# A fused delta-rule attention and GELU feed-forward kernel, rebuilt: batches in partition halves, a Newton inverse, 512-token feed-forward groups, casting weight loads

## The chip, the cores and the metric

The kernel runs on one core of a Trainium2 chip. The metric is the device time of one execution in microseconds (us). "Slower", "faster" and "same" compare it with the kernel before on the same chip. All profile times are from the start of the profiled span.

## The reference

Two stages follow each other. `q`, `k`, `v` are `[4, 8, 768, 48]` (batch, head, position, head size), `beta` is `[4, 8, 768]`.

```python
k_n = k / (np.linalg.norm(k, axis=-1, keepdims=True) + 1e-06)
for t in range(S):                          # state: [B, H, 48, 48], zero at first
    y[:, :, t] = einsum('bhd,bhde->bhe', q[:, :, t], state)
    v_old = einsum('bhde,bhd->bhe', state, kt)
    state = state + bt * einsum('bhd,bhe->bhde', kt, vt - v_old)
x = y.transpose(0, 2, 1, 3).reshape(3072, 384)
h = x @ w_in                                # [384, 2048]
g = 0.5 * h * (1 + tanh(c * (h + 0.044715 * h**3)))
out = g @ w_out                             # [2048, 384]
```

Both kernels cut the 768 positions into 12 chunks of 64. Within a chunk the recurrence is a triangular system: with the strictly lower matrix A of `beta_i k_i.k_j`, the updates of a chunk are `U = (I + A)^-1 (beta V - beta K state)`, the new state is `state + K^T U`, and the output is `Q state + tril(Q K^T) U`.

## The kernel before, in words

Work is cut into 24 units. Unit `u` is chunk `u // 2` of two of the four batches, so 16 (batch, head) pairs, laid out as 8 column groups on two partition halves of 64 (`pairs`, L293): the two halves hold two heads of one batch. Matrices of one pair are 64x64, so nearly every matmul uses one 64x64 tile of TensorE, and two of them run side by side on the diagonal tiles.

A unit has three parts, all in functions of the kernel's body:

- `prep(u)` (L398): POOL squares `k`, takes the norm (`pow`, L415), scales `k` by it and by `beta` (L411 to L427); TensorE turns the three 64x64 blocks of a pair (48 transposes, L435), DVE copies them out (L438); `gram2` and `gram` (L455, L448) form the triangular matrices, which DVE masks (L462, L466). The inverse of `I + A` is a product of `I + A^(2^i)`: L474 to L541 square a matrix five times and apply it, with three right-hand blocks in `mnl`, `m4`, `n4`, `m5` and `lt`. `wmat` (L543) makes `beta K` times the inverse.
- `chain(u)` (L554): the serial part, from one chunk's state to the next: `umat` (L566), `smat` (L584), the state's sum (L594), `omat` (L597). The output comes out with head dimension on partitions, 48 of each 64; six small DMAs on SP's queue (L616) move the fourth group of heads into the 16 free rows, so that `xo` holds the 384 features as three blocks of 128.
- `mlp(u)` (L620): for 128 tokens, 48 matmuls of 128 columns against `W1` (L633), GELU on ACT (L638, four 512-column pieces), 16 matmuls of 384 columns against `W2` (L645), a copy and two output DMAs.

`W1` and `W2` come in float32 through two staging buffers `wst` on SP's queue (L381) and are cast by ACT or DVE (L386) into bf16. `load(c)` (L361) brings a chunk of `k`, `q`, `v` for all four batches; three buffers (`NR`). Five `prep` buffers (`NP`), four of `xo` (`NX`).

The order is made by a planner in `Flow.schedule` (L70): each operation has an estimated duration and a key (its due time in units, `prep` at `u`, `chain` at `u - 0.5`, `mlp` from `u + 2.5`). The planner simulates the engines, takes at each free engine the ready operation with the lowest key, places PSUM tiles in 8 banks, and so fixes every engine's queue; `emit` (L167) writes the queues with semaphore waits. TensorE's queue is in order: an operation that waits holds all behind it.

Of the kernel before, what the change touches and what calls it, by code (L numbers as in the profile page):

```python
# [8 lines left out]
BF16 = mybir.dt.bfloat16  # L9
ALU = mybir.AluOpType  # L10
# [8 lines left out]
class Op:  # L19
    __slots__ = ("engs", "fn", "dur", "key", "deps", "alloc", "frees", "mode", "dma", "users", "missing",  # L20
                 "on", "t0", "t1", "tag", "clock", "bankdeps", "seq")


class Flow:
# [3 lines left out]
    LAT = {"pe": 0.20, "dve": 0.08, "act": 0.08, "pool": 0.10}  # L28
    SWITCH = 0.095
    SLACK = 0.6  # L30
    DMA_LAT = 2.2

# [7 lines left out]
    def add(self, eng, fn, dur, reads=(), writes=(), key=0.0, alloc=None, accum=(), frees=(), mode=None, dma=None):  # L40
        o = Op()
        o.engs = (eng,) if isinstance(eng, str) else tuple(eng)
        o.fn, o.dur, o.key, o.mode, o.dma = fn, dur, key, mode, dma
# [6 lines left out]
        for name in o.frees:  # L50
            self.left[name] += 1
# [18 lines left out]
    def schedule(self):  # L70
# [17 lines left out]
        events, t, done, mode, dma_free = [], 0.0, 0, None, 0.0  # L88

# [6 lines left out]

        def choose(e):
            held, pick = [], None
            while ready[e]:
                item = heapq.heappop(ready[e])  # L100
                o = item[2]
                if o.on is not None:
                    continue
                held.append(item)
                if pick is not None and item[0] - pick[0] > self.SLACK:
                    break
                if o.alloc and place(o.alloc[1]) is None:
                    continue
                if e != "pe" or o.mode == mode:
                    pick = item  # L110
                    break
                if pick is None:
                    pick = item
            for item in held:
                if item is not pick:
                    heapq.heappush(ready[e], item)
            return pick[2] if pick else None

        while done < len(self.ops):
            for e in ENGINES:  # L120
                while free[e] <= t + 1e-9:
# [5 lines left out]
                    if e == "pe" and o.mode != mode:  # L127
                        d += self.SWITCH
                        mode = o.mode
# [6 lines left out]
                    if o.dma is not None:  # L136
                        dma_free = max(dma_free, t + 0.65) + d
                        free[e], o.t1 = t + 0.65, dma_free + self.DMA_LAT
# [8 lines left out]
            while True:  # L147
                if o is not None:
                    done += 1
                    for name in o.frees:  # L150
                        self.left[name] -= 1
                        b = self.at[name]
                        for x in range(b, b + self.size[name]):
                            last[x].append(o)
                            if not self.left[name]:
                                bank[x], since[x] = None, t
# [8 lines left out]
        self.t_end = t  # L165

    def emit(self, nc, psum):  # L167
        count, total, names = {e: 0 for e in ENGINES}, {}, list(ENGINES)
        last_done, groups = {}, {}
# [12 lines left out]
        plan = {e: [] for e in ENGINES}  # L182
        for o in sorted(self.ops, key=lambda o: (o.t0, o.seq)):
            e, mine = o.on, known[o.on]
            need = {}
            for d in o.deps | o.bankdeps:
                if d.on == e and d.dma is None and (e == "pe" or self.only_war(o, d)):
                    continue
# [44 lines left out]
    def only_war(self, o, d):  # L233
        return False


def bass_deltanet__then__act_gelu_tanh_kernel(
# [12 lines left out]
    NC, FC, G, J = S // C, FF // 128, 8, 4  # L250
    NU = 2 * NC
    DP = 112
# [4 lines left out]
    with nc.allow_non_contiguous_dma("strided loads"), nc.allow_low_precision("bf16 pipeline"):  # L257
# [5 lines left out]
        NR, NP, NX = 3, 5, 4  # L263
        ident = sb("ident", [128, 128], F32)
        id64 = sb("id64", [128, C])
        mfull = sb("mfull", [128, 2, 128], F32)
        mneg = sb("mneg", [128, C], F32)
        mup = sb("mup", [128, 2, C], F32)
        half = sb("half", [128, G], F32)
        braw = sb("braw", [32, NC, 2, C], F32)  # L270
        bsb = sb("bsb", [128, NC, 2 * G], F32)
        raw = {n: sb(n + "raw", [128, 2 * G, D], F32, NR) for n in "kvq"}
        sq = sb("sq", [128, G, D], F32)
        nrm = sb("nrm", [128, 4, G], F32, NP)
        kn, kb, qb = (sb(n, [128, G, C], BF16, NP) for n in ("kn", "kb", "qb"))
        vb = sb("vb", [128, G, D], BF16, NP)
        kT = sb("kT", [128, 3, G, C], BF16, NP)
        mnl = [sb(f"mnl{i}_", [128, 3, G, C], BF16, NP) for i in range(3)]
        m4, n4, m5, lt = (sb(x, [128, G, C], BF16, NP) for x in ("m4", "n4", "m5", "lt"))
        wn = sb("wn", [128, G, C], BF16, NP)  # L280
        us = sb("us", [128, G, D], BF16, 3)
        st = sb("st", [128, G, D], BF16, 4)
        xo = sb("xo", [128, J, 128], BF16, NX)
        gT = sb("gT", [128, FC, 128], BF16, 3)
        ob = sb("ob", [128, DM], F32, 2)
        W1 = sb("W1", [128, 3, FF])
        W2 = sb("W2", [128, FC, DM])
        wst = sb("wst", [128, FF], F32, 2)

        def half_rows(a, n=C):  # L290
            return slice(64 * a, 64 * a + n)

        pairs = [(g, a) for g in range(G) for a in range(2)]  # L293
        PEO, T1, T2 = 0.05, 0.0165, 0.029


        def const():
            A("pool", lambda e, P: e.memset(ident[:, :], 0.0), 0.2, writes=["ident"])
            A("pool", lambda e, P: e.affine_select(out=ident[:, :], in_=ident[:, :], compare_op=ALU.not_equal, fill=1.0,
                                                   base=0, pattern=[[-1, 128]], channel_multiplier=1), 0.4,  # L300
              reads=["ident"], writes=["ident"])
            A("pool", lambda e, P: e.memset(half[:, :], 0.5), 0.1, writes=["half"])
            A("pool", lambda e, P: e.memset(mfull[:, :, :], -1.0), 0.3, writes=["mfull"])
            for x, cm in ((0, 1), (1, -1)):
                A("pool", lambda e, P, x=x, cm=cm: e.affine_select(
                    out=mfull[:, x, :], in_=mfull[:, x, :], compare_op=ALU.is_gt, fill=0.0, base=0,
                    pattern=[[-cm, 128]], channel_multiplier=cm), 0.4, reads=["mfull"], writes=["mfull"])
            for a in range(2):
                r = half_rows(a)
                A("dve", lambda e, P, r=r: e.tensor_copy(id64[r, :], ident[r, r]), 0.15, reads=["ident"],  # L310
                  writes=[f"id64{a}"])
                A("dve", lambda e, P, r=r: e.tensor_copy(mneg[r, :], mfull[r, 0, r]), 0.25, reads=["mfull"], writes=[f"mneg{a}"])
                A("dve", lambda e, P, r=r: e.tensor_copy(mup[r, 0, :], mfull[r, 1, r]), 0.25, reads=["mfull"], writes=[f"mupa{a}"])
                A("dve", lambda e, P, r=r: e.tensor_scalar(mup[r, 1, :], mfull[r, 1, r], -1.0, None, op0=ALU.mult), 0.2,
                  reads=["mfull"], writes=[f"mupb{a}"])

        ID = ["id640", "id641"]
        MNEG, MUP = ["mneg0", "mneg1"], ["mupa0", "mupa1", "mupb0", "mupb1"]
# [4 lines left out]
        def ev(n, wide=False):  # L323
            return {"act": 0.18 + 0.00083 * n, "dve": 0.14 + (0.00053 if wide else 0.00104) * n}

        EV = ("act", "dve")
        PAD = lambda s: [f"pad{s}", f"pad{s}.1", f"pad{s}.2"]

        def warm_up():
            wz = sb("wz", [128, 128])  # L330
# [371 lines left out]
```

## Time and profile before

| what | value |
|---|---|
| three runs | 385.56, 392.3, 393.79 us (median 392.3) |
| profiled execution | 392.4 us span |
| TensorE matmuls in it | 10,020, each with a weight load |
| granted TensorE clock, mean | 0.970 |
| HBM read, written | 20.55 MB, 4.72 MB |

PE is TensorE's matmul, PEld its weight load, DVE is VectorE, ACT ScalarE, POOL GpSimd, SP SyncE. A busy digit is tenths of a slice. The end of a matmul is modelled, so the time from the start of one operation to the start of the next is the better price of a matmul on a full TensorE. The queue row "instruction" is the fetching of program code: most of its packets hold 16,384 bytes.

### The profile page before, as it was taken

The numbers are of one execution on the slowest core, as the hardware profiler recorded it, in microseconds if no ns is written. First come the engines' busy times: TensorE is split into PE (matmuls) and PEld (weight loads), VectorE is DVE, ScalarE is ACT, GpSimd is POOL, SyncE is SP. The second block draws the span as 40 slices with busy tenths as digits, with TensorE's granted clock in tenths as the row PEclk, the third lists the DMA queues.
The fourth block names the chain that finished last, engine by engine and source line by source line (L and its number), as shares of the span: only waits on it lengthen the run. The fifth ranks groups of instructions, "written<-read, shape, count | busy, mean of one in ns | idle before, by whom it ended". The sixth has DMA issues, their size and how long they took to land.

```text
span 392.4 us, 21411 instructions
## 1 busy us (share of the span) xinstructions
PE 333.6 (85%) x10020; PEld 277.5 (71%) x10020; DVE 234.0 (60%) x387; ACT 188.2 (48%) x327; POOL 165.8 (42%) x203
## 2 busy tenths in 40 slices
PE   4346846867999999988988998999998998999966
PEld 4346845756778777767776787788877886887744
DVE  6756836746767576474664773776577565556300
ACT  1034326456555545545544455556635664564522
POOL 8973733769688318234434436343322211011000
PEclk9999968899999999998999999999999999999988
DMA  9999996890651163053035033010111110101110
GB/s 141 169 163 160 176 187 97 159 190 12 161 113 39 24 107 65 8 103 64 6 71 90 15 67 67 5 28 7 25 26 26 26 23 7 28 6 39 31 24 20
DMA packets 86600, 27.23 MB, mean 69 GB/s; under 512 B 81008, under 2 KB 86128, under 8 KB 86128
## 3 DMA queue, kind: packets, MB, share of 16 engines
q1 hardware_dynamic: 82816, 25.18, 36.0%
q8 instruction: 78, 1.28, 1.4%
q10 hardware_dynamic: 3696, 0.69, 1.2%
q14 instruction: 10, 0.08, 0.1%
HBM read 20.55 MB, written 4.72 MB: 64 GB/s over the span
## 4 chain that ended last, share of the span: by engine, by line
PE 63%; issue 9%; DVE 8%; POOL 7%; SPq 6%; DMA 5%; ACT 2%; ACTq 0%; POOLq 0%
PE ps L633 14%; PE ps L645 13%; PE ps L493 7%; SPq L616 5%; PE ps L487 5%; PE ps L435 4%; POOL nrm L415 3%; PE ps L524 3%; PE ps L478 3%; PE ps L451 2%; DMA xo<-xo 2%; DMA kraw<-in_k_dram 2%; PE ps L572 2%; PE ps L458 2%; PE ps L545 2%
## 5 line engine op out<-in xcount | busy, mean ns | idle before, releaser
L633 PE MATMUL ps<-xo,W 128*128 128x128 bf16 x1152 | 81.3, 224 | 11.5 <-DMA xo<-xo 7.7
L638 ACT ACTIVATE gT<-ps 128x512 bf16<-128x512 f32 x96 | 57.3, 597 | 70.2 <-PE ps L633 69.0
L633 PEld LDWEIGHTS ps<-xo,W 128*128 128x128 bf16 x1152 | 69.7, 100 | 20.2 <-DMA xo<-xo 9.2
L645 PE MATMUL ps<-W,gT 128*128 128x384 bf16 x384 | 77.8, 329 | 0.0
L321 ACT ACTIVATE mnl<-ps 128x512 bf16<-128x512 f32 (+1 forms) x75 | 52.8, 710 | 48.1 <-PE ps L478 28.7
L470 POOL TENSOR_TENSOR mnl<-mnl,id 128x512 bf16<-128x512 bf16 x24 | 27.7, 1156 | 105.9 <-DVE mnl L466 102.7
L493 PE MATMUL ps<-mnl 64*64 64x128 bf16 x1152 | 49.0, 228 | 7.1 <-issue 6.0
L321 DVE CAST mnl<-ps 128x512 bf16<-128x512 f32 (+1 forms) x45 | 33.0, 734 | 30.5 <-PE ps L487 17.3
L415 POOL TENSOR_TENSOR nrm<-nrm,half 128x8 f32<-128x8 f32 x24 | 39.8, 1658 | 13.9 <-DVE nrm L413 13.8
L493 PEld LDWEIGHTS ps<-mnl 64*64 64x64 bf16 x1152 | 38.2, 115 | 8.9 <-issue 7.0
L645 PEld LDWEIGHTS ps<-W,gT 128*128 128x128 bf16 x384 | 31.3, 98 | 17.3 <-issue 0.5
L539 DVE TENSOR_TENSOR lt<-ps,lt 128x384 bf16<-128x384 f32 (+1 forms) x48 | 23.4, 488 | 31.8 <-PE ps L524 31.1
L518 DVE TENSOR_TENSOR mnl<-ps,mnl 128x512 bf16<-128x512 f32 x48 | 32.9, 686 | 9.6 <-ACT mnl L321 9.3
L487 PE MATMUL ps<-mnl 64*64 64x64 bf16 (+1 forms) x1152 | 32.9, 198 | 4.5 <-ACT mnl L321 2.4
L427 POOL TENSOR_TENSOR vb<-vraw,bsb 128x384 bf16<-128x384 f32 x23 | 20.0, 869 | 35.8 <-PE ps L577 29.7
L487 PEld LDWEIGHTS ps<-mnl 64*64 64x64 bf16 x1152 | 26.1, 115 | 9.0 <-ACT mnl L321 2.3
L466 DVE TENSOR_TENSOR mnl<-ps,mup 128x1024 bf16<-128x1024 f32 x24 | 29.2, 1219 | 0.7 <-PE ps L451 0.6
L438 DVE COPY kT<-ps 112x1536 bf16<-112x1536 bf16 x24 | 22.8, 952 | 8.0 <-PE ps L435 7.9
L524 PE MATMUL ps<-lt,m 64*64 64x48 bf16 (+1 forms) x768 | 21.5, 187 | 6.3 <-issue 5.8
L411 POOL TENSOR_TENSOR sq<-kraw 128x384 f32<-128x384 f32 x22 | 18.7, 849 | 15.5 <-DMA kraw<-in_k_dram 15.5
L524 PEld LDWEIGHTS ps<-lt,m 64*64 64x64 bf16 x768 | 17.2, 113 | 11.1 <-issue 8.0
L420 POOL TENSOR_TENSOR kn<-kraw,nrm 128x384 bf16<-128x384 f32 x23 | 19.1, 828 | 11.6 <-DVE nrm L419 9.3
(82 smaller groups left out, 551.1 us busy)
## 6 DMA issues: line engine op xcount, KB each, us to landing
out_dram<-ob SPq DMA_DIRECT2D x48, 96.0 KB, 2.4
kraw<-in_k_dram SPq DMA_DIRECT2D x22, 192.0 KB, 5.5
qraw<-in_q_dram SPq DMA_DIRECT2D x22, 192.0 KB, 5.6
vraw<-in_v_dram SPq DMA_DIRECT2D x22, 192.0 KB, 4.7
wst<-in_moe_w_out_dram SPq DMA_DIRECT2D x4, 768.0 KB, 5.9
wst<-in_moe_w_in_dram SPq DMA_DIRECT2D x6, 384.0 KB, 7.4
xo<-xo SPq DMA_DIRECT2D x144, 4.0 KB, 2.2
wst<-in_moe_w_in_dram SPq DMA_DIRECT2D x6, 128.0 KB, 8.1
```

Of the source, the lines that this page charges most:

```text
L321: return e.activation(out, in_, ACT.Copy) if e is nc.scalar else e.tensor_copy(out, in_)
L415: A("pool", lambda e, P: e.tensor_tensor(nr[:, 1, :], nr[:, 0, :], half[:, :], ALU.pow), 1.65, reads=[n("nrm"), "half"], writes=[n("nrm")] ...
L466: A("dve", lambda e, P: e.tensor_tensor(z0[:, 1:3, :, :].rearrange("p x g t -> p g x t"), P(ps("G")).rearrange("p (g x t) -> p g x t", x=2 ...
L470: A("pool", lambda e, P: e.tensor_tensor(z1[:, 2, :, :], z0[:, 1, :, :], id64[:, :].unsqueeze(1).to_broadcast([128, G, C]), ALU.add), 1.16 ...
L487: ins = e.matmul(cols(P, name, 0, g, w)[r, :], z[r, 1, g, :], z[r, 0, g, 0:w])
L493: ins = e.matmul(cols(P, name, 0, 2 * g, 2 * C)[r, :].rearrange("p (x t) -> p x t", x=2), z[r, 0, g, :], z[r, 1:3, g, :])
L518: A("dve", lambda e, P, z=z, pn=pn, lout=lout: e.tensor_tensor(lout, g2(P, pn, 1), z[:, 2, :, :], ALU.add), 0.69, reads=[n(zn + "l"), afte ...
L524: ins = e.matmul(cols(P, name, 0, g, C - lo, lo)[r, :], m[r, g, :], lt[s][r, g, lo:C])
L539: A("dve", lambda e, P, lo=lo, pl=pl: e.tensor_tensor(lt[s][:, :, lo:C], P(pl).rearrange("p (g t) -> p g t", g=G)[:, :, lo:C], lt[s][:, :, ...
L633: ins = e.matmul(P(ph)[:, 128 * f:128 * f + 128], W1[:, t, 128 * (i + f):128 * (i + f) + 128], x_[:, t, :], start=(t == 0), stop=(t == 2))
L638: A("act", lambda e, P, i=i, ph=ph: e.activation(g_[:, i:i + 4, :].rearrange("p f t -> p (f t)"), P(ph), ACT.Gelu_apprx_tanh), 0.62, frees ...
L645: ins = e.matmul(P(po)[:, 0:DM], g_[:, f, :], W2[:, f, :], start=(f == 0), stop=(f == FC - 1))
```

## The change

The new kernel computes the same with the same 24 units and the same planner class.

- **Layout.** A partition half is now a batch, the free dimension holds the 8 heads. A pair of heads lies side by side in 128 columns, so one 128x128 transpose turns two heads of two batches: 12 instead of 48 (L446). `gram`, `gram2` and the products with the state use all four 64x64 corners of the array (`quad`): a head's parity picks the row half, the batch the column half.
- **Inverse.** The power product is replaced by five Newton steps, X <- X(2I - LX), each two products: the first with -L (or its transpose, in turn), to which DVE adds 2I (L515), the second with X, and a copy of the result (L520). In steps 1 and 3 (`WIDE`) the two halves are one block-diagonal 128x128 operand, `bd`, filled by POOL (two `affine_select` in step 1, two copies in step 3) and used by 8 matmuls instead of 16. Masking is by `copy_predicated` (L474, L478) onto preset buffers. `wmat`, the apply steps and POOL's L470 are gone.
- **Chain.** `K state` is subtracted from `v` by DVE (L550), then `umat` multiplies with the inverse; `Q state` and the inner product share a PSUM tile `O` of two banks. The output has tokens on partitions; three 128x128 transposes (L596) put the features there. The six copying DMAs are gone.
- **Feed-forward.** Tokens are taken in groups (`GROUPS`): chunks 0, 1, 10 and 11 alone (256 tokens), the others two by two (512 tokens). An up matmul has 256 or 512 columns; a GELU instruction covers 1,024 columns, two PSUM banks.
- **Weights.** Four DMAs on POOL's queue cast float32 to bf16 on the way; W1's wait for chunk 0's `v`, W2's for chunk 1's `v`. The staging buffers and the 24 casts go.
- **Planner.** It models code blocks of 256 instructions with a refill of 4.2 us, gives ACT first call on the copies that DVE could also do, and makes POOL wait between operations on different partition halves. The clearing of PSUM by DVE (L656, 3,472 ns) goes, and TensorE's warm-up is 24 matmuls of 512 columns.

```diff
-        pairs = [(g, a) for g in range(G) for a in range(2)]
+        quad = [(p, a) for a in range(2) for p in range(2)]
+    WIDE = (1, 3)
+    GROUPS = [[0], [1]] + [[c, c + 1] for c in range(2, NC - 2, 2)] + [[NC - 2], [NC - 1]]
...
+                A("pool", lambda e, P, f0=f0: e.dma_start(W1[:, :, f0:f0 + FF // 2], w1v[:, :, f0:f0 + FF // 2]), 7.0,
+                  reads=["vraw01"], writes=[f"W1{i}"], dma=f"w1{i}", key=-3 + 0.1 * i)
...
+                for y in range(3):
+                    for g in range(4):
+                        c0 = 512 * y + 128 * g
+                        ins = e.transpose(t[:, c0:c0 + 128], tok[s][:, y, 2 * g:2 * g + 2, :]..., ident[:, :])
...
+            def gram(e, P):
+                for g in range(4):
+                    for p, a in quad:
+                        r = hf(p, D)
+                        o = P(ps("G"))[hf(a), 512 * p + 128 * g:512 * p + 128 * g + 128]
+                        ins = e.matmul(o..., kT[s][r, 1, g, hf(a)], kT[s][r, 0:3:2, g, hf(a)])
...
+            A("dve", lambda e, P: e.copy_predicated(
+                wp[s][:, :, :], mup[:, :].bitcast(U16).unsqueeze(1).to_broadcast([128, H, 2 * C]),
+                P(ps("G")).rearrange("p (h t) -> p h t", h=H)), 1.24, ...)
...
+            for i in range(1, 6):
+                def product(e, P, name, cur=cur, wide=wide, rhs=None):
+                    for h in range(H):
+                        o = P(name)[:, C * h:C * h + C]
+                        if wide:
+                            ins = e.matmul(o, bd[s][:, h, :], rhs[:, h, :])
+                        else:
+                            for a in range(2):
+                                ins = e.matmul(o[hf(a), :], cur[hf(a), h, :], rhs[hf(a), h, :])
...
+                A("dve", lambda e, P, i=i: e.tensor_tensor(rt[s], P(ps(f"A{i}")), two, ALU.add), 0.71, ...)
...
-            for t in range(3):
                 for a in range(2):
-                    A("sp", lambda e, P, t=t, a=a: e.dma_start(x_[64 * a + 48:64 * a + 64, t, :],
-                                                               x_[64 * a + 16 * t:64 * a + 16 * t + 16, 3, :]),
...
+            def trans(e, P):
+                for j in range(J):
+                    ins = e.transpose(P(ps("X"))..., xb[:, 128 * j:128 * j + 128], ident[:, :])
...
+            nf = 1024 // w
+            for i in range(0, FC, nf):
+                def up(e, P, i=i, ph=ph):
+                    for f in range(nf):
+                        for j in range(J):
+                            ins = e.matmul(P(ph)[:, w * f:w * f + w], W1[:, j, 128 * (i + f):...], x_[:, j, 0:w], ...)
```

Line numbers of the new functions are those of the changed kernel.

649 lines of the change are left out of this document (309 added, 340 removed).

## The prediction

> **What bounds the kernel now.** I read the page's busy line and slices first, then the busy times by stretch, then TensorE's timeline inside one stretch, last the chain of work.
>
> ```profile
> PE 333.6 (85%) x10020; PEld 277.5 (71%) x10020; DVE 234.0 (60%) x387; ACT 188.2 (48%) x327; POOL 165.8 (42%) x203
> ...
> PE   4346846867999999988988998999998998999966
> ...
> DMA  9999996890651163053035033010111110101110
> ...
> q8 instruction: 78, 1.28, 1.4%
> ```
>
> TensorE is the only engine that fills slices, and only from 100 us on. Before that the DMA engines are full and TensorE is not.
>
> ```profile
> 0.00:60.00 60.00, 32.96 (x987) 30.42 (x988) 38.43 (x63) 15.79 (x26) 41.48 (x74) 0.94 1.07 167
> 60.00:100.00 40.00, 29.86 (x1009) 26.44 (x1010) 25.07 (x46) 22.97 (x40) 26.25 (x26) 0.91 0.63 117
> 100.00:240.00 140.00, 129.35 (x3842) 104.94 (x3838) 88.78 (x154) 71.10 (x126) 66.70 (x71) 0.99 0.34 65
> 240.00:360.00 120.00, 116.20 (x3763) 96.38 (x3760) 76.59 (x117) 65.37 (x114) 31.36 (x35) 1.00 0.10 21
> 360.00:392.40 32.40, 25.23 (x439) 19.35 (x437) 5.14 (x8) 13.00 (x24) 0.00 (x0) 0.89 0.12 27
> ```
>
> Columns: stretch, PE, PEld, DVE, ACT, POOL busy with counts, clock, DMA share, GB/s. A unit has 416 matmuls (272 prep, 80 chain, 64 feed-forward). From 240 to 360 us 3,763 matmuls are 9.05 units: 13.26 us a unit, with TensorE busy 97%. At that rate 24 units are 318 us; the other 74 us of the span are lost: in the first 100 us only 1,996 matmuls run (4.8 units, worth 64 us, so 36 lost), from 100 to 240 some 18 (3,842 are 9.2 units, 122 us), the rest at the end.
>
> ```profile
> 252.07 0.83 PE L633 MATMUL ps<-xo,W 128*128 128x128 bf16 x12
> 252.84 0.42 PE L524 MATMUL ps<-lt,m 64*64 64x32 bf16 x16
> 253.11 0.42 PE L487 MATMUL ps<-mnl 64*64 64x64 bf16 x16
> 253.36 0.61 PE L493 MATMUL ps<-mnl 64*64 64x128 bf16 x16
> 253.81 0.40 PE L545 MATMUL ps<-lt,kb 64*48 64x64 bf16 x16
> 254.14 0.82 PE L645 MATMUL ps<-W,gT 128*128 128x384 bf16 x4
> 254.80 0.83 PE L633 MATMUL ps<-xo,W 128*128 128x128 bf16 x12
> ...
> 256.84 0.38 PE L587 MATMUL ps<-us,kn 64*48 64x48 bf16 x16
> ```
>
> Start to start gives the prices: 16 diagonal matmuls of 64 columns 0.25 us, of 128 columns 0.45 to 0.49, 12 full ones of 128 columns 0.77 (64 ns each), 4 of 384 columns 0.66 (0.43 ns a column). The smallest group, L587, takes 0.22 until 257.06.
>
> ```profile
> 25.77 4.47 issue
> ...
> 49.62 5.78 issue
> ...
> 378.65 1.71 DMA xo<-xo
> ```
>
> In the chain of work, "issue" is TensorE waiting for nothing that the profile names. The queue "instruction" moved 78 packets for 20,040 matmuls and loads, 257 a packet, and 30 packets in the 120 us from 240 on: one in 4.0 us. I read the issue pieces as waits for code behind the full DMA engines. The last line is the end: the copy of heads inside `xo`, waited out by the last unit.
>
> **The change part by part.** All per unit, on TensorE, at the prices above.
> - *Transposes*: 48 small ones (0.76) become 12 full ones, 12 x 64 ns = 0.77.
> - *Grams*: 0.25 + 0.45 before. Now four corners. The warm-up (L338) is the only row of that: 20 matmuls of 64 columns on the diagonal in 5.26:5.77 (0.51 us), then 34 counted on four corners in 5.77:6.11 (0.34). So corners cost between half and all of the diagonal; I take 0.26 for each gram (half of 0.49 for 128 columns, and for 64 columns no better than the diagonal), 0.52; upper end 0.74.
> - *Inverse*: before 0.51 (L478) + 3 x (0.26 + 0.49) + 0.27 + 2 x 0.34 + 0.33 = 4.0. Now 6 narrow products of 16 x 64 columns, 6 x 0.26 = 1.56, and 4 wide ones of 8 matmuls with a full weight load and 64 columns. No row has that shape: at half of the full 128-column matmul 8 x 32 ns = 0.26, at the whole of it 0.51. I take 0.27, since a wide one streams half the columns and L633's loads already keep pace with 64 ns; 1.08, upper end 2.04. Sum 2.64.
> - *Chain*: before 0.53 + 0.22 + 0.55 = 1.30. Now two products with the state (0.22 each by L587), `umat` and `omat` 0.26 each, `smat` 0.22, three transposes 0.20: 1.38; nothing saved. The six DMAs go. They cost SP 0.59 us each and 1.71 until landing at the end, and hold up the up matmuls 9.2 us in the list of waits.
> - *Feed-forward*: up 4 x 0.77 = 3.08 before. Now 48 matmuls of 512 columns at 0.43 ns, 10.6 us for four units, 2.65; with 256-column groups the same. Down unchanged, 4 x 0.68 = 2.72. The whole gain of the wide groups is 0.4.
>
> Sum now 0.77 + 0.52 + 2.64 + 1.38 + 5.37 = 10.7, against 12.6 for the old parts by the same prices. The old kernel needed 13.26, that is 1.05 times, for waits; 10.7 x 1.05 = 11.2. Twenty-four units: 270 us against 318.
>
> *Code*: 6,828 matmuls instead of 10,020 (255 a unit outside the feed-forward, 768 in it, 36 at the start), 53 packets; one in 5.0 us of TensorE's work instead of 4.0. The Trainium skill, "Runtime: NRT & Kernel Launch", "Instruction fetch mechanics", holds that fetching is hidden behind the issue of instructions. Here it is not (4.47 and 5.78 us above), so a shorter program is worth something.
>
> A rule against the change: the Trainium skill, "TensorE: Matmul & The Clock Gate" ("Wait — 56ns, not 53.3ns?"), says that matmuls never start closer than about 25 ns. By it the 240 small matmuls of a unit would take 6.0 us instead of 4.3, and the estimate from that page is 40 us more, 355. L487's 16 in 0.25 us are 16 ns apart, so I sum by the row.
>
> *Other engines, per unit.* DVE: reduce 0.53, two small ones 0.4, kT 0.95, masks, five sums with 2I at 0.69 (L518's size) = 3.4, two chain sums 1.1. For `copy_predicated` the trace has no row; L462 and L466 read the same PSUM tiles and take 0.69 and 1.22. Below that I see no reason to go, since the reads are the same; above, twice: 1.9 to 3.8; I take 1.9. DVE 8.3 us of 11.2. ACT: GELU 2 x 1.02 (a 128x1024 ACTIVATE takes 1,024 ns), copies 5 x 0.60 + 4 x 0.49: 7.0, of which DVE takes some. POOL: 0.85 + 1.64 + 0.83 + 0.83 + 0.58, two `affine_select` of 512 elements (128 elements took 0.28 to 0.59; 0.6 to 2.0 each, I take 0.9) and two copies (0.4 each): 7.3, at most 10. All lie beside TensorE; if TensorE were free, DVE would be next at some 10 us with its share of the copies. What is late behind them is hidden by five prep buffers: a unit's five Newton steps are 5 x (0.26 + 0.2 + 0.7 + 0.26 + 0.2 + 0.6) = 11 us and POOL's fills, some 25 us from norm to inverse, against 5 x 11.2.
>
> *The start.* The loads are as many bytes, 9.8 MB up to three chunks and both weights, at 167 GB/s 59 us. In the old kernel the weights queue behind chunks on SP and behind two staging buffers: the last cast of W is at 111 us, and SP issues the first `xo` copies only at 56 us for an `omat` of 44 us, so the first up matmul is at 78 us. Now weights run on their own queue, W1 at some 30 to 40 us, W2 by 60. POOL's presets (15 small memsets 0.2, eight to ten selects, some 13 us) come ahead of its first `pow`, which was at 6.9 us; the first unit's transposes slip from 14 to some 18, its inverse to 40, feed-forward from about 48 us. Until then TensorE has four units' prep, some 17 us of work, and a wait for code or two. Lost: 34 us, then no more than the 5%.
>
> W1's and W2's waits stand in POOL's queue: if chunk 1's `v` lands late, `pow` and the scalings of the next units stand behind W2's issue, and TensorE has nothing to do but W1's matmuls. The planner lets W1 go first, so some 5 us of that are in the 34.
>
> *The end.* After the last matmul 0.49 us of copy and the output DMA, 3.7 us as before (388.7 to 392.4). The last group's feed-forward is counted above; its last GELU and the chain ahead of it leave TensorE waiting some 3 us, and part at half clock as before (0.89 over 360:392). 7 us, against the old 11.
>
> Sum: 270 + 34 + 7 = 311, and 4 for copies that come late with DVE at three quarters: 315. The profiled execution's own span is 392.4, the median of the runs 392.3, so nothing is added.
>
> **The rivals.**
> - *VectorE becomes the bound.* If `copy_predicated` costs twice and DVE takes two copies a unit: 8.3 + 1.9 + 1.3 = 11.5, at 95% 12.1 x 24 = 290, from 15 us on, plus 18 for the last group's feed-forward and output, plus 15 of waits in the chain: 338. For it: DVE has 76.6 of 120 us now and gets more; against: ACT is at 65 and gets first call on the copies.
> - *TensorE's pieces are dearer:* wide products and corners at their upper ends, 10.7 + 0.96 + 0.22 + 0.2 = 12.1 x 1.05 x 24 = 305, + 45 = 350.
> - *Little is lost*: no waits in the steady part (257), 28 at the start, 7: 292.
> - *Slower: casting loads land late.* No casting DMA is in the trace. Nearest are the rows of W's loads (768 KB in 5.9 us) and the 4-byte packets, some 10 ns each, a bound of a few GB/s if a cast moved single elements. Before W2 lands, TensorE can do the chains of chunks 0 to 3 (three `xT` buffers), five units' prep and two groups of up matmuls, some 75 us. Then 195 us remain and 7 at the end: the old time is reached when W2 lands at 190 us, 6.3 MB at under 36 GB/s from 15 us on; +2% at 198. Against: 167 GB/s with 192-byte packets. The Trainium skill, "DMA: Bandwidth & Descriptors" ("SWDGE vs HWDGE vs iDMA"), adds that such loads have their descriptors written by GpSimd into SBUF, which DVE can lock out; no run here shows it.
>
> **How the numbers follow.** TensorE-bound as summed, 298 to 330: 0.57. Little lost: 0.12. VectorE or dear pieces, 330 to 360: 0.22. Late weights 0.09, of which 0.04 beyond 400 and 0.02 within 2% of now. The range 294 to 350 leaves out some 0.2. Faster by over 2% 0.94, within 2% 0.02, slower 0.04; 2% is about what a measurement of this kernel tells from no change.
>
> **What would show it.** Start to start in the timeline: products of 16 in 0.26 us, wide ones in 0.27, six up matmuls of 512 columns in 1.32. PE busy over 90% from about 55 us on, first up matmul before 55, W2's landing by 65. "instruction" at some 53 packets and fewer issue pieces after 60 us. `copy_predicated` at 0.7 and 1.2. I am wrong if DVE, not PE, fills the middle slices, if POOL shows a wait for a DMA of over 8 us, or if TensorE waits for copies over 10% of the middle.

## The result, and the profile after

The changed kernel takes 334.09 us (median of four runs, 330.74 to 336.52) beside 392.22 for the kernel before on the same chip: a ratio of 0.862, 95% interval 0.855 to 0.869. Forecast: 315, range 294 to 350. Its profiled execution took 330.74 us with a span of 329.0. An execution over 1.5% above the quickest of its kernel counts as slow and enters no ratio, and three of the four of the kernel before lie that far above its 385.56; the profiles of e1, e4 and e8 came from such executions too, so no lengths are compared from them. The two medians alone give 334.09 / 392.22 = 0.852; the ratios of the experiments, taken beside a kernel before of 390.6 to 392.9 us (medians, on four chips), are to be set against that number.

From the page of the changed kernel: the busy line, the slices, the code queue, the prices of new operations (count, busy us, mean ns), and the weights' DMAs (KB, us from issue to landing).

```profile
PE 291.2 (89%) x6809; PEld 203.8 (62%) x6828; DVE 217.5 (66%) x362; ACT 148.9 (45%) x239; POOL 166.5 (51%) x252
...
PE   8246786979999788999989999989999999999994
...
DVE  5887689774789999764894574985657766652000
...
PEclk9855596799999999999999999999999999999999
DMA  9999976764625633201511112301012100011221
...
q8 instruction: 53, 0.87, 1.1%
...
L624 ACT ACTIVATE gT<-ps 128x1024 bf16<-128x1024 f32 x48 | 49.2, 1024 | 38.0 <-PE ps L619 37.9
L496 POOL COPY bd<-xi 64x256 f32<-64x256 f32 x48 | 18.9, 394 | 55.0 <-ACT xi L329 46.9
...
L490 POOL TENSOR_SCALAR_AFFINE_SELECT bd<-ln 64x512 bf16<-64x512 bf16 x48 | 31.5, 655 | 25.2 <-DVE ln L474 21.4
...
L478 DVE CAST_PREDICATED wp<-mup,ps 128x1024 bf16<-128x1024 uint16 x24 | 29.2, 1216 | 0.3 <-PE ps L462 0.3
...
W<-in_moe_w_in_dram POOLq DMA_DIRECT2D x2, 768.0 KB, 9.6
W<-in_moe_w_out_dram POOLq DMA_DIRECT2D x2, 768.0 KB, 18.5
```

A slice is 8.2 us. TensorE's slices are at 7 or more from the eighth on (58 us), where the old one got there from its tenth on (88 us). Two dents stay: the first 58 us, partly at half clock (the 5s of PEclk), and the 7 and 8s from 107 to 131 us, where DVE shows 9s.

The busy times by stretch (same columns as in the prediction) put numbers on that.

```profile
0.00:60.00 60.00, 39.41 (x789) 29.45 (x790) 45.38 (x79) 13.94 (x24) 48.21 (x87) 0.70 0.98 155
60.00:100.00 40.00, 37.62 (x853) 28.55 (x851) 29.28 (x58) 20.07 (x31) 38.39 (x44) 0.98 0.53 104
100.00:140.00 40.00, 34.40 (x1147) 25.57 (x1146) 36.77 (x66) 22.35 (x38) 32.84 (x46) 1.00 0.44 83
140.00:160.00 20.00, 19.79 (x442) 12.69 (x444) 11.63 (x20) 8.36 (x15) 4.79 (x7) 1.00 0.17 37
160.00:240.00 80.00, 76.92 (x1932) 51.36 (x1935) 54.35 (x83) 40.80 (x66) 30.19 (x48) 1.00 0.17 36
240.00:300.00 60.00, 58.63 (x1422) 40.31 (x1419) 37.97 (x55) 32.45 (x51) 12.10 (x23) 1.00 0.09 21
300.00:329.00 29.00, 24.43 (x270) 15.87 (x267) 2.12 (x4) 10.88 (x18) 0.00 (x0) 0.99 0.19 45
```

From 100 to 140 us DVE is busy 36.8 of 40 us and TensorE 34.4: there the order is turned round. Everywhere after 140 us TensorE is the full engine.

TensorE's timeline from the steady stretch shows the pieces, to be read from start to start.

```profile
244.56 0.81 PE L632 MATMUL ps<-W,gT 128*128 128x384 bf16 x4
245.21 0.40 PE L507 MATMUL ps<-rt,bd 128*128 128x64 bf16 x8
245.54 0.44 PE L510 MATMUL ps<-ln,xi 64*64 64x64 bf16 x16
245.91 0.82 PE L632 MATMUL ps<-W,gT 128*128 128x384 bf16 x4
246.66 0.44 PE L510 MATMUL ps<-ln,xi 64*64 64x64 bf16 x16
...
248.06 0.44 PE L510 MATMUL ps<-rt,xi 64*64 64x64 bf16 x16
248.33 0.42 PE L510 MATMUL ps<-wp,xi 64*64 64x64 bf16 x16
248.68 0.82 PE L632 MATMUL ps<-W,gT 128*128 128x384 bf16 x4
249.44 0.32 PE L470 MATMUL ps<-kT 48*64 48x64 bf16 x16
249.58 0.40 PE L462 MATMUL ps<-kT 48*64 48x128 bf16 x16
249.91 0.82 PE L632 MATMUL ps<-W,gT 128*128 128x384 bf16 x4
```

Four L632 take 0.65 us when a full-row operation follows (244.56 to 245.21), and 0.75 and 0.76 when one on 64-row tiles does (245.91, 248.68). A product of 16 (L510) takes 0.27 before another, 0.35 to 0.37 before a full one. So a change between the full array and 64-row tiles costs about 0.1 us, either way. Over all such pairs the median gap beyond streaming is 96 to 111 ns for these changes and 7 to 14 ns between diagonal and four-corner tiles. The Trainium skill, "TensorEngine Tiling (Array Packing)", "Key Properties", says that changing the tiling mode drains TensorE; the trace shows a gap at these changes too, of this size.

**The account.** I priced each part from load to load in 160 to 300 us, waits included, up matmuls by their width. The forecast's prices stand beside it (without its factor of 1.05).

| part, us a unit | forecast | measured |
|---|---|---|
| transposes | 0.77 | 0.73 |
| grams | 0.52 | 0.58 |
| inverse | 2.64 | 3.31 |
| chain | 1.38 | 1.55 |
| up | 2.65 | 2.79 |
| down | 2.72 | 2.66 |
| sum | 10.7, times 1.05 = 11.2 | 11.62 |

Some expectations below quote 11.3 for this price; there all up matmuls were counted alike, and their counts of units differ a little from those here. Counting every matmul at these prices tells how many units of work a stretch holds; what is left of the stretch is lost. Lost us:

| kernel (span) | 0 to 60 | 60 to 100 | 100 to 140 | 140 to 300 | rest | sum |
|---|---|---|---|---|---|---|
| changed (329.0) | 39.2 | 2.7 | 4.4 | -1.5 | 5.2 | 50.0 |
| e2 (329.8) | 40.1 | -0.4 | 5.7 | -0.6 | 6.1 | 50.9 |
| e3 (329.4) | 34.6 | 3.4 | 6.9 | 0.8 | 4.9 | 50.5 |
| e7 (329.4) | 37.9 | 0.7 | 7.2 | -0.2 | 4.6 | 50.4 |
| e9 (320.7) | 38.7 | 1.0 | 1.3 | -3.3 | 4.2 | 41.9 |
| e12 (324.9) | 43.0 | 1.4 | 1.2 | -3.7 | 4.0 | 45.9 |

With 24 x 11.62 = 279 each row adds up to its span. Negative means that TensorE did better there than the price. The changed kernel's row is that of its quickest execution, 3.4 us below its median, so what e2 and e3 gained over it by their medians (2.5 us) isn't in these rows.

**The late first feed-forward.** The first up matmul starts at 70.9 us, not before 55. ACT's and its DMA queue's lines show one reason:

```profile
31.58 0.60 ACTq L404 DMA_DIRECT2D vraw<-in_v_dram  x1
...
47.70 0.59 ACT L329 ACTIVATE xi<-ps 128x512 bf16<-128x512 f32 x1
...
62.16 0.52 ACT L540 ACTIVATE rs<-vraw 128x384 bf16<-128x384 f32 x1
```

Unit 1's inverse is copied out at 47.70, but its right side, the negated `v` of L540, runs only at 62.16, because that half of `v` is issued at 31.58 and its copy was ordered late. The description of the change and the prediction have this dependency the wrong way round: `weights()` stands before `load()` in program order, so a weight DMA that "reads" `vraw01` makes the load of `v` wait for the weight, and the weight waits for nothing.

### The profile page after: what moved, and what is told of

Read it like the earlier page. It is cut to its first block, busy times and chain, and to the rows that moved or that the text cites. A ratio compares the mean times of both kernels' runs of the same rounds, so it can differ in the third digit from the quotient of the medians.

```text
span 329.0 us, 14919 instructions
## 1 busy us (share of the span) xinstructions
PE 291.2 (89%) x6809; PEld 203.8 (62%) x6828; DVE 217.5 (66%) x362; ACT 148.9 (45%) x239; POOL 166.5 (51%) x252
## 4 chain that ended last, share of the span: by engine, by line
PE 55%; POOL 25%; DVE 11%; issue 4%; ACT 2%; DMA 1%; POOLq 0%
PE ps L632 15%; PE ps L619 15%; PE ps L510 10%; POOL nrm L436 8%; PE ps L507 6%; POOL bd L490 4%; PE ps L451 3%; POOL tok L441 3%; DVE rt L515 3%; POOL sq L433 3%; DVE kT L454 3%; POOL bd L496 2%; ACT xi L329 1%; PE ps L546 1%; POOL tok L443 1%
## 5 line engine op out<-in xcount | busy, mean ns | idle before, releaser
L515 DVE TENSOR_TENSOR rt<-ps,two 128x512 bf16<-128x512 f32 x120 | 80.7, 686 | 34.3 <-PE ps L510 29.2
L329 ACT ACTIVATE xi<-ps 128x512 bf16<-128x512 f32 x99 | 58.6, 596 | 91.1 <-PE ps L507 48.1
L632 PE MATMUL ps<-W,gT 128*128 128x384 bf16 x384 | 75.1, 327 | 0.4 <-ACT gT L624 0.4
L619 PE MATMUL ps<-xT,W 128*128 128x256 bf16 (+1 forms) x365 | 66.0, 323 | 2.4 <-issue 1.4
L624 ACT ACTIVATE gT<-ps 128x1024 bf16<-128x1024 f32 x48 | 49.2, 1024 | 38.0 <-PE ps L619 37.9
L619 PEld LDWEIGHTS ps<-xT,W 128*128 128x128 bf16 x384 | 34.4, 98 | 18.9 <-ACT xT L329 0.5
L490 POOL TENSOR_SCALAR_AFFINE_SELECT bd<-ln 64x512 bf16<-64x512 bf16 x48 | 31.5, 655 | 25.2 <-DVE ln L474 21.4
L632 PEld LDWEIGHTS ps<-W,gT 128*128 128x128 bf16 x384 | 32.2, 98 | 17.6 <-ACT gT L624 0.6
L510 PE MATMUL ps<-rt,xi 64*64 64x64 bf16 x1152 | 31.7, 198 | 1.3 <-DVE rt L515 1.3
L510 PEld LDWEIGHTS ps<-rt,xi 64*64 64x64 bf16 x1152 | 24.6, 112 | 12.9 <-DVE rt L515 5.8
L451 PE MATMUL ps<-ident,tok 128*128 128x128 bf16 x288 | 23.2, 239 | 8.8 <-DVE tok L443 8.6
L478 DVE CAST_PREDICATED wp<-mup,ps 128x1024 bf16<-128x1024 uint16 x24 | 29.2, 1216 | 0.3 <-PE ps L462 0.3
L451 PEld LDWEIGHTS ps<-ident,tok 128*128 128x128 bf16 x288 | 19.2, 108 | 11.2 <-DVE tok L443 9.0
L507 PE MATMUL ps<-wp,bd 128*128 128x64 bf16 x384 | 20.8, 201 | 5.8 <-POOL bd L496 3.9
L510 PE MATMUL ps<-ln,xi 64*64 64x64 bf16 x768 | 21.5, 200 | 3.6 <-ACT xi L329 3.3
L510 PEld LDWEIGHTS ps<-ln,xi 64*64 64x64 bf16 x768 | 16.9, 114 | 8.8 <-ACT xi L329 5.8
L507 PE MATMUL ps<-rt,bd 128*128 128x64 bf16 x384 | 20.6, 201 | 1.2 <-DVE rt L515 1.1
## 6 DMA issues: line engine op xcount, KB each, us to landing
W<-in_moe_w_out_dram POOLq DMA_DIRECT2D x2, 768.0 KB, 18.5
```

What stands on the lines that cost most here:

```text
L329: return e.activation(out, in_, ACT.Copy) if e is nc.scalar else e.tensor_copy(out, in_)
L451: ins = e.transpose(t[:, c0:c0 + 128], tok[s][:, y, 2 * g:2 * g + 2, :].rearrange("p h d -> p (h d)"), ident[:, :])
L478: A("dve", lambda e, P: e.copy_predicated(wp[s][:, :, :], mup[:, :].bitcast(U16).unsqueeze(1).to_broadcast([128, H, 2 * C]), P(ps("G")).re ...
L490: A("pool", lambda e, P, src=src, dst=dst: e.affine_select(out=dst, in_=src, compare_op=ALU.not_equal, fill=1.0, base=0, pattern=[[0, H], ...
L507: ins = e.matmul(o, bd[s][:, h, :], rhs[:, h, :])
L510: ins = e.matmul(o[hf(a), :], cur[hf(a), h, :], rhs[hf(a), h, :])
```

## The experiments

Times are medians. Units done are counted as above.

**e1: the weights don't name `v`.**

```diff
-                  reads=["vraw01"], writes=[f"W1{i}"], dma=f"w1{i}", key=-3 + 0.1 * i)
+                  writes=[f"W1{i}"], dma=f"w1{i}", key=-3 + 0.1 * i)
...
-                  reads=["vraw11"], writes=[f"W2{i}"], dma=f"w2{i}", key=-2 + 0.1 * i)
+                  writes=[f"W2{i}"], dma=f"w2{i}", key=-2 + 0.1 * i)
```

> The changed kernel, with the two reads of v taken off the four casting loads. In program order the loads of v are added after the weights, so these reads make v (chunk 0 and 1, second pair of batches) wait for the weights to land, not the weights for v; now neither waits. Theory V (late v is what the start lost beyond the forecast): v of unit 1 lands before 15 us, first up matmul at 50 to 56 us instead of 71, and 8 to 16 us off, 318 to 326. Rival P (POOL's queue, busy 48 of the first 60 us and 38 of the next 40, sets the start anyhow): first up matmul no earlier than 62 us, 0 to 4 us off.

Measured: 337.06 us, ratio 0.861 (0.856 to 0.866), no faster than the changed kernel. The late `v` is real, but taking it away is worth nothing by itself. Theory V's 8 to 16 us didn't come.

**e2: `v` first.** The loads of chunks 0 and 1 are put ahead of the weights, so that the weights wait for `v` as the text had it.

```diff
+        load(0)
+        load(1)
         weights()
...
-            if u % 2 == 0:
+            if u % 2 == 0 and u >= 4:
```

> The changed kernel with the loads of chunks 0 and 1 added before the weights, so that W1 waits for v of chunk 0 and W2 for v of chunk 1, as the prediction had read it. Theory V: the same gain as with no wait at all, within 4 us; W2 lands later (by 10 us at most), which costs nothing if it is there by 60 us. Rival P: 0 to 4 us off; a wait of POOL for v over 5 us long would show in POOL's list and make it slower than the changed kernel.

Measured: 331.62 us, ratio 0.847 (0.841 to 0.852). The first up matmul comes at 55.0, 16 us sooner, and the time falls by 2.5. By 100 us 5.19 units are done (changed kernel: 5.00), by 140 us 8.15 (8.05): the early feed-forward fills a stretch that was nearly full, and is missing from 100 to 140, where 5.7 us are lost now. e2 is 5.4 us faster than e1 on the same chip, so Theory V's "same gain as with no wait at all, within 4 us" fails as well. The two differ in whether the weights wait for `v`, and in the order in which the loads are added; e12 comes back to that.

**e3: the weights in float32 through two staging buffers and 24 casts, as before the change** (three `ob` buffers for four, to make room).

```diff
+        wst = sb("wst", [128, FF], F32, 2)
...
-                A("pool", lambda e, P, f0=f0: e.dma_start(W1[:, :, f0:f0 + FF // 2], w1v[:, :, f0:f0 + FF // 2]), 7.0, ...)
+            for j in range(J):
+                stage([(0, FF // 2, w1v[:, j, 0:FF // 2]), (FF // 2, FF, w1v[:, j, FF // 2:FF])], W1[:, j, :], FF, -1.5 + 0.1 * j, ...)
```

> The changed kernel with the weights loaded as before the change: float32 through two staging buffers on SP's queue, cast by ACT or DVE (three output buffers instead of four, for space). Theory C (the casting loads are what starts the feed-forward early): last cast of W2 after 80 us, 8 to 15 us slower than the changed kernel, 342 to 349. Rival V: the staged loads do not hold v, so what is lost on the weights is won on v: within 4 us of the changed kernel.

Measured: 331.63 us, ratio 0.847 (0.843 to 0.851). 2.19 units by 60 us, the best start of all (34.6 lost); by 140 us 8.19, little more than elsewhere. Theory C falls: the casting loads bring this kernel nothing, for e2, where `v` isn't late either, takes 331.62.

**e4: only the casting loads, in the kernel before.**

```diff
-                stage(parts, W1[:, t, :], FF, -1.5 + 0.1 * t, f"W1{t}")
+                for rows, src in parts:
+                    A("pool", lambda e, P, t=t, rows=rows, src=src: e.dma_start(W1[rows, t, :], src), 1.2, ...)
...
-                stage([(slice(0, 128), w2v[:, i:i + 4, :])], ...)
+                A("pool", lambda e, P, i=i: e.dma_start(W2[:, i:i + 8, :], w2v[:, i:i + 8, :]), 7.0, ...)
```

> The kernel before, with casting loads on POOL's queue in place of staging and casts: this part of the change alone. Theory C: the feed-forward's start no longer waits for W (last cast at 111 us), 24 casts of 0.5 us gone, SP's queue shorter so that the first copies inside xo go earlier: 8 to 15 us off 392, 377 to 384. Rival: the first up matmul (78 us) hangs on those copies behind the chunk loads, not on W, and POOL's issues of descriptors come before its pow: 0 to 4 us off.

Measured: 389.8 us against 391.72, ratio 0.992 (0.987 to 0.997). Of the change's 58 us this part alone brings 2 to 3, not the 8 to 15 of Theory C.

**e5, e6, e7: which engine sets the time?** The changed kernel with more work for one engine in each unit: six matmuls of 512 columns (1.3 us, 31 in all), three DVE memsets (0.5 each, 36), three POOL memsets (0.52 each, 37).

```diff
+            def extra(e, P):
+                for j in range(6):
+                    ins = e.matmul(P(ps("E"))[:, :], ident[:, :], wz[:, :])
+                return ins
+            A("pe", extra, 1.3, reads=[n("kT"), "ident", "wz"], alloc=(ps("E"), 1), frees=[ps("E")], mode="m", key=u, mm=6)
```

```diff
+            for j in range(3):
+                A("dve", lambda e, P, j=j: e.memset(scr[j][:, :], 0.0), 0.5, reads=[n("kT")], writes=[f"scr{j}"], key=u)
```

(e7 has the same three lines on "pool", at 0.52.)

> The changed kernel with work added to TensorE alone: in each unit, after kT, one group of six 512-column matmuls into a PSUM bank of its own that nobody reads, 1.3 us, 31 us in all. Theory F (TensorE is the bound from about 60 us to the end, and the first stretch is paced by prep, into whose gaps feed-forward is only filled): of 24 groups the 5 or 6 in the first 60 us cost nothing, the others full price, +22 to +28 us over 334. Rival D (DVE and POOL pace the kernel up to 140 us, ten units): +12 to +18.

> The changed kernel with work added to DVE alone: three memsets of 128x512 float32 a unit into scratch, some 0.5 us each, 1.5 us a unit, 36 us in all. Theory F: DVE is 66% busy, so 0 to +5 us. Rival D: DVE was 92% busy from 100 to 140 us; +8 to +15.

> The changed kernel with work added to POOL alone: three memsets of 128x512 bf16 a unit into scratch, 0.52 us each, 1.6 us a unit, 37 us in all. Theory F: 0 to +3 us. Rival D: POOL was 38 of 40 us busy from 60 to 100 us; +8 to +15.

Measured: e5 352.39 (ratio 0.905, 0.899 to 0.910), 18 of 31 us; e6 344.23 (0.884, 0.877 to 0.890), 10 of 36; e7 328.54 (0.844, 0.837 to 0.851), 5.6 less than without the extra work. Set against 0.852, the ratios make that 21 and 12 more and 3 less, so these differences are good to some 3 us. e5 lies between Theory F and Rival D, e6 where Rival D had it, e7 with neither. TensorE is the engine that counts most; POOL is not the bound, though it is busy 38.4 of 40 us from 60 to 100. e6 loses early: 6.96 units by 140 us instead of 8.05, worth 12.7 us. From 160 to 300 us, 12 of its 24 groups of memsets run, 17.5 us of VectorE, and 12.06 units are done against 12.15, the same rate. In e5 11 of the 24 groups of matmuls run there, 15.3 us of TensorE from load to load, and 11.12 units are done, 12.0 us less work. So VectorE's work counts until 140 us, and TensorE's after. e7 also gives a scale: another duration in the planner moves the order, and the order alone is worth some 3 to 5 us. Any run here brings a new order with it, and so an unplanned part of that size.

**e8: norms first.** e2, with POOL's fills and the issues of the weights placed behind the first norms.

```diff
-            key = 0.25 * s - 6
+            key = -0.03
...
-                A("pool", lambda e, P, n=n: e.memset(tok[s][:, n, :, D:C], 0.0), 0.25, writes=[f"tok{n}{s}"], key=key - 2)
+                A("pool", lambda e, P, n=n: e.memset(tok[s][:, n, :, D:C], 0.0), 0.25, writes=[f"tok{n}{s}"], key=s - 0.4)
...
-                  reads=["vraw01"], writes=[f"W1{i}"], dma=f"w1{i}", key=-3 + 0.1 * i)
+                  reads=["vraw01"], writes=[f"W1{i}"], dma=f"w1{i}", key=0.9 + 0.1 * i)
```

(W2 likewise, from -2 to 1.2.)

> The kernel of e2 (v before the weights) with POOL's fills and the issues of the weight loads put behind the first units' norms by their keys, so that the first pow comes at some 7 us instead of 15.6. Theory H (each us taken off the way of the first unit to its inverse comes off the end): 5 to 8 us off e2's 331.6, 324 to 327. Rival: rates, not the first unit's way, set the end; within 2 us of e2.

Measured: 331.02 us, ratio 0.847 (0.838 to 0.856), e2 again. In its profiled execution the first `pow` starts at 10.5 us (e2: 14.3), not at some 7, and the first unit's U comes 3.3 us sooner. So Theory H's 5 to 8 us didn't come; 3 us would be within the interval, and the theory is neither borne out nor ruled out.

After these eight the start could be bettered in several ways, and little of the gains was left at 140 us (8.05 units in the changed kernel, 8.11 to 8.19 in e2, e3 and e7). That made the stretch before 140 the suspect: the units' feed-forward is taken by TensorE as soon as it can, and the prep of units 6 to 11 then comes in one burst (transposes of units 6 to 11 at 92 to 123 us in the changed kernel, up matmuls at 70.9 to 91 and none again until 128), DVE full and TensorE without other work. The next three are all made from e2.

**e9: feed-forward due two units later.**

```diff
-            key, span = 2 * g[-1] + 3.0, 2.0 * len(g)
+            key, span = 2 * g[-1] + 5.0, 2.0 * len(g)
```

> The kernel of e2_v_first (331.62 us), with the due time of a feed-forward group two units later (2*g[-1]+5.0 for 2*g[-1]+3.0), so that the prep of units 6 and 7 goes ahead of the feed-forward of chunks 0 and 1 and the two kinds of work share the stretch from 100 to 140 us. Theory B (bursts: in that stretch TensorE lacks feed-forward work, and VectorE is full of prep): units done there rise from the 2.5 of e2 to 2.9 or more, VectorE falls below 33 of 40 us, and the time falls by 4 to 9, to 323 to 328. Rival N (the stretch is short because everything behind it waits for the same preps, in whatever order): units done by 160 us stay at 9.9 +- 0.2, time 329 to 335.

Measured: 323.17 us, ratio 0.826 (0.820 to 0.832), 8.5 less than e2. One line of e2's busy times, and then those of e9:

```profile
100.00:140.00 40.00, 35.09 (x1110) 26.91 (x1116) 35.76 (x61) 21.67 (x36) 27.99 (x40) 0.91 0.39 73
```

```profile
100.00:140.00 40.00, 37.22 (x1104) 26.73 (x1103) 36.21 (x65) 20.17 (x34) 32.42 (x45) 1.00 0.44 82
140.00:160.00 20.00, 19.00 (x521) 12.59 (x521) 15.85 (x33) 10.85 (x19) 16.76 (x18) 1.00 0.23 43
160.00:240.00 80.00, 79.52 (x2025) 52.82 (x2020) 57.82 (x86) 42.34 (x69) 29.43 (x48) 1.00 0.16 36
240.00:300.00 60.00, 60.00 (x1234) 39.47 (x1231) 29.63 (x44) 31.39 (x48) 7.11 (x14) 1.00 0.09 22
```

3.33 units are done from 100 to 140 us instead of 2.95, the clock stays at 1.00, and TensorE is busy 139.5 of the 140 us from 160 on. Theory B holds in time; its count for e2 was 2.5, so in units only the rise compares, 0.38 for 0.4 or more. Its figure for VectorE fails (36.2 us, not below 33): VectorE isn't spared, TensorE has feed-forward to do beside it. e2 runs no up matmul from 86 to 128 us, e9 some at 94 to 101 and at 120 to 131. By the account 4.4 us are won in the stretch itself, 2.7 from 140 to 300 and 1.9 at the end. Up to 3.6 of the 4.4 can be the clock (0.09 of 40 us); but at a clock of 1.00 the changed kernel loses 4.4 us there too. How much of the rest is the order at large (3 to 5 us by e7) isn't shown.

**e10: every feed-forward group of one chunk.**

```diff
-    GROUPS = [[0], [1]] + [[c, c + 1] for c in range(2, NC - 2, 2)] + [[NC - 2], [NC - 1]]
+    GROUPS = [[c] for c in range(NC)]
```

> The kernel of e2_v_first with all feed-forward groups of one chunk (256 tokens): undoes the 512-token groups. Theory W (the wide matmul is worth what it saves on TensorE): up matmuls of 256 columns cost as much a column (0.42 ns) as those of 512, so nothing is lost on TensorE beyond 0.1 us a unit, and a chunk's feed-forward can start two units earlier, which gives TensorE something between the preps in 100 to 140: 326 to 331. Rival L (more weight loads and more starts of groups cost 0.2 to 0.4 us for each of 16 units, 3 to 6 us): 334 to 338.

Measured: 336.13 us, ratio 0.860 (0.854 to 0.865): 4.5 more than e2, where Rival L had it, but not by its reason. An up matmul of 256 columns costs 118 ns and one of 512 costs 231, so a unit's up part is 2.82 us or 2.78: the width is worth nothing there. The stretch from 100 to 140 gains (3.23 units for 2.95), and 160 to 300 loses a little (11.96 for 12.05). The profiled span is 2.9 us longer than e2's, and the account puts the loss at the end: 10.8 us after 300 us, against 6.1 in e2. Why the end is longer stays open.

**e11: all five Newton steps wide.**

```diff
-    WIDE = (1, 3)
+    WIDE = (1, 2, 3, 4, 5)
```

> The kernel of e2_v_first with all five Newton steps wide (block-diagonal 128x128 operand), where the change has steps 1 and 3: six products of a unit become 8 full-row matmuls at 30.6 ns (0.245 us) for 16 diagonal ones at 13 to 16 ns (0.22 us), POOL gets six more copies of 0.4 us a unit. Theory S (a change between full-row and 64-row tiles costs TensorE 0.1 us): the changes in 160 to 300 us fall from some 155 to under 110, 0.3 to 0.4 us a unit less, the price of a unit there 11.3 to 10.9, and 5 to 9 us off the time, 323 to 327. Rival P (the longer way of a step through POOL, 0.9 us more in three steps, shows in the preps of 60 to 140): 332 to 340 whatever the changes cost.

Measured: 333.86 us, ratio 0.854 (0.848 to 0.860). The changes of tile from 160 to 300 us fall from 160 (e2) to 109, as Theory S said, but the price hardly follows: 12.19 units for 12.05, 0.13 us a unit less where Theory S had 0.3 to 0.4. The wide matmuls, some 30 ns when alone, stand at 44.7 ns there with all that lies between them (39.5 in e2), 3.57 us for the inverse; POOL's fills of `bd` are waited for 2.2 us in that stretch. And 1.45 units are done by 60 us (1.71), 2.63 from 100 to 140 (2.95): each step's longer way through POOL, as Rival P said, and the time is in its range.

**e12: e9 with weights that wait for nothing.** In e9 the first inverse is held up at its first product. The list of waits of its first 60 us, one line for POOL's queue and one for TensorE (us in total, times, longest):

```profile
POOL W L417 <- DMA vraw<-in_v_dram: 8.7, 1, 8.7
```

```profile
PE ps L507 <- POOL bd L490: 8.8, 2, 8.5
```

The fill of `bd` stands behind the issue of W2 in POOL's queue, and that one waits for `v` of chunk 1. e12 takes the `reads` off both weights, as e1 did.

> The kernel of e9_later_ff (323.17 us) with the order of loads kept and without the weights' waits for v. In e9 POOL's issue of W2 waits 8.7 us for chunk 1's v (16.7 to 25.5 us), and the first unit's bd fill stands behind it, so that TensorE's first Newton product waits 8.5 us, until 30.1. Theory Q (POOL's queue sets the start, now that the stretch behind it is no longer limited by bursts): first Newton product at 22 to 25 us, first U by 42 instead of 47.3, and the time falls by 3 to 6, to 317 to 320. Rival D (the bytes set the start: 155 GB/s and DMA engines 99% busy until 60 us, so that with weights sooner the k, q and v of chunks 1 and 2 come later): first product sooner, units done by 60 us still 1.8 +- 0.15, time 321 to 326.

Measured: 328.43 us, ratio 0.841 (0.836 to 0.846), 5.3 more than e9. The same two lists in e12:

```profile
POOL sq L433 <- DMA kraw<-in_k_dram: 10.5, 1, 10.5
```

```profile
PE ps L507 <- POOL bd L490: 9.8, 1, 9.8
```

The first product starts at 25.5 instead of 30.1, but with 6.3 MB of weights ahead of it the next chunk's `k` lands late (33.1 and 36.3 us; e9: 25.6 and 27.3), POOL waits for that in its square of a later unit, and the second unit's `bd` fill stands behind it. The first unit's U is at 52.9 (e9: 47.3), and 43.0 us are lost until 60, 4.3 more than in e9, as much as the spans differ. Theory Q falls; D had the direction and too small a size.

```profile
0.00:60.00 60.00, 31.12 (x671) 22.22 (x672) 40.62 (x69) 11.55 (x20) 40.27 (x77) 0.72 0.98 156
```

With DMA engines 98% busy until 60 us (e12's row), the wait for `v` did good: it let the chunks through first.

e9 is the best version, 323.17 us.

## Why the prediction was right, and where its sum was wrong

The main claim held: TensorE stays the bound (e5, e6), and fewer and fuller matmuls shorten its work. Of the 63 us between the two profiled spans 39 are the price of a unit, 13.26 to 11.62, and 24 are time lost beside it, 74 to 50; forecast were 48 and 29. How much the new layout, the Newton inverse and the chain bring each is not shown: no run takes one of them out. The measured case is "TensorE-bound as summed"; the median lies 4 us above that case's own range of 298 to 330. It is nearer to the 338 of the VectorE rival than to 315, but that is chance: that rival's condition, `copy_predicated` at twice its price, didn't come.

Forecast 270 + 34 + 7 + 4 = 315; the profiled span is 279 + 39.2 + 5.2 + 5.6 = 329. So the median is 315 and 9 for the price, 5 for the start, 2 for the middle, less 2 for the end, and 5 between the profiled span and the median.

- *Transposes, grams, chain, down.* Within 0.2 us of the forecast each. That four corners take half of the diagonal's time held: L470, 16 matmuls of 64 columns, 0.14 us (taken: 0.26, too dear), L462 with 128 columns 0.2 and the change after it.
- *Inverse: 2.64 forecast, 3.31 measured.* The term of the sum that was mis-sized; 0.67 of the 0.92 us by which the parts are dearer than 10.7. The pieces themselves are right (wide ones 8 x 30 ns = 0.24 for 0.27, narrow ones 0.27 for 0.26). What is missing, I think, is the change of tile: wide, narrow and feed-forward operations alternate, 155 changes in the 12.15 units from 160 to 300 us, 12.8 a unit at 0.1 us or more. The old kernel had 97 in 9.05 units, 10.7 a unit, so their number alone rose little; but the sum priced a narrow product beside its like (253.11 to 253.36), where no change follows, and an old up group (252.07 to 252.84) with the change in it. Waits for other engines are not it: at the inverse's products they are 1.0 us in that whole stretch. The "dear pieces" rival had the place and the wrong reason: not the streaming of wide matmuls, but what lies between them. That the changes are the cause is argued from the gaps and not shown: e11, which took a third of them away, lowered the price of a unit by 0.13 us alone.
- *Up: 2.65 forecast, 2.79 measured*, and e10 bears out that the width of the groups brings nothing.
- *The start: 34 forecast, 39.2 measured.* Its parts went otherwise. W1 and W2 were issued at 11.8 and 13.6 us and took 9.6 and 18.5 to land, sooner than forecast (30 to 40, and 60). The step that failed is "feed-forward from about 48 us": 70.9, by the `v` that waits for the weights, which I read the wrong way round. It cost little (e2: 2.5 us). Half clock, 0.50 from 20 to 40 us against 1.00 in the old kernel (third column from the right below, changed kernel first), was not in the sum; its share was not tried.

```profile
20.00:40.00 20.00, 13.07 (x273) 10.73 (x271) 14.87 (x25) 2.99 (x5) 18.04 (x24) 0.50 1.17 179
```

```profile
20.00:40.00 20.00, 11.82 (x316) 10.61 (x312) 12.54 (x20) 7.79 (x13) 11.40 (x12) 1.00 1.09 164
```

- *The middle: 4 forecast, 5.6 measured* (2.7 + 4.4 - 1.5). "Copies that come late" was right as a name; what they hide behind was not. "What is late behind them is hidden by five prep buffers" fails from 100 to 140 us, where preps come in a burst: e6 shows that DVE's work counts up to there, and e9 that another order spreads the burst.
- *The end: 7 forecast, 5.2 measured.* The chain's last lines are matmuls without a wait between them, then 4.4 us of copy and output:

```profile
313.96 5.41 PE ps L619 x48
319.37 5.21 PE ps L632 x32
```

- *Other durations.* `copy_predicated` 1.22 us as taken, `affine_select` 0.66 (taken 0.9), `bd` copies 0.39 (0.4), GELU 1.02, 53 code packets (53). So VectorE as the bound was rightly a rival for the whole, and true for one stretch of 40 us.
- *Late casting loads* were no danger: 768 KB in 9.6 to 18.5 us. They are no gain here either (e3), and 2 to 3 us in the old kernel (e4).
- *The signs.* Of those that were to show the forecast wrong none came: DVE is ahead of TensorE in one stretch alone, POOL's longest wait for a DMA is 1.2 us, and TensorE's waits from 100 to 300 us are some 10 us, 5%. Of those for it, "first up matmul before 55" failed and "W2's landing by 65" came (35 us).
- *Nothing added to the span* was wrong by 1.7 us (330.74 for 329.0), and the median lies 3.4 above the profiled run.

## What to carry to other kernels

Price a TensorE-bound change by its pieces from start to start, and add the changes between full and 64-row tiles as a term of their own, some 0.1 us each. When a better start is gone again by a fixed time, look for the burst in that stretch: spreading two kinds of work by one number of the order was worth 8.5 us here, and no repair of the start more than 3; but any new order can bring 3 to 5 by itself. A wait in a queue can be a throttle that lets more urgent bytes through; look at what it holds back before taking it out.

## What the runs showed of the hardware that was not expected

- A change between full-row and 64-row tiles leaves a gap of 96 to 111 ns (median) on TensorE; between diagonal and four-corner tiles 7 to 14 ns.
- Four-corner matmuls follow each other at 8 ns with 64 columns (L470) and some 13 ns with 128 (L462); a full-row matmul of 64 columns (L507) takes some 30 ns.
- The granted clock was 0.50 from 20 to 40 us, though 24 matmuls of 512 columns had run until 10 us. TensorE then waited for `tok` until 19.20 (8.55 us), and was busy 13.07 of the 20 us at half clock.
- With the DMA engines full, TensorE waited in the old kernel for nothing that the profile names 4.47 us until 30.24 and 5.78 until 55.40; in the new one two such waits are left in the first 70 us, 0.83 until 49.97 and 0.97 until 66.50. They stand at multiples of some 128 matmuls, as one code packet in 257 instructions would have it; that they are waits for code is read from that and not shown otherwise.
